# A token over two PSUM banks, six casts moved to ScalarE, three subtractions moved to GpSimd, and other banks for the row turns, in a fused attention and expert kernel

## The chip, the cores and the metric

The kernel runs on one core of one Trainium2 chip. The metric is device time in microseconds (us) of one execution. TensorE (PE) multiplies and turns tiles into PSUM, VectorE (DVE), ScalarE (ACT) and GpSimd (POOL) do the elementwise work, SyncE (SP) issues most DMAs. Each engine works through its own instructions strictly in order.

## The reference

Windowed attention over 4 batches of 576 positions and 8 heads gives 2304 rows of 512. A top-1 mixture of 8 experts works on the rows, then a dense layer.

```python
scores = scale * q @ k.T + slopes * -abs(rel)        # window of 128 back
x = softmax(scores) @ v                               # 2304 rows of 512
logits = x @ w_gate + modality_bias[modality_id]
e = argmax(logits); gate = softmax(logits)[e]
y[e == i] = gate * (maximum(x[e == i] @ w1[i], 0) @ w2[i])    # w1: 512 x 1024
r = maximum(y @ w_in, 0)                              # w_in: 512 x 2048
out = (r * r) @ w_out
```

## The kernel before

All large products run on TensorE in a split form: each fp32 operand becomes a high part (a cast to fp32r) and a low part (the operand minus the high part), and three of the four part products are added in PSUM (`passes`, L691). PSUM has 8 banks, given out by tag: two each for s, t and v, one each for x and m. Where a tag has two banks they are taken in turn, so a new tile waits until the tile before the last of that tag has been read out.

**Order.** The program is written as one stream under a manual schedule, so the order in the code is the order on each engine. Helpers written as generators are advanced one step at a time at fixed places; a `yield` in one moves what follows to a later place.

**Attention** runs in 40 units (batch, 128 queries, half of the heads). In step k, VectorE makes the scaled and biased scores of unit k (`smax`, L274 to L281), ScalarE their exponentials (L300), TensorE the scores of unit k+1 (`sc`, banks s and t, L258 or L260), the transposes of unit k-2 (`tr`, a bank of v, L322) and the products with v of unit k-3 (`pv`, bank x, L359). ScalarE reads the transposes out (`ev`, L329 to L335), and GpSimd masks them (L339, L340). After every second unit `post` copies the finished rows from bank x (ScalarE, L379), turns them back together with the gate products (TensorE, L388) and scales them (VectorE, L403).

**Routing** (`route`) handles two or three row tiles at a time in steps that are taken between `tr` and `pv`, and once more behind `pv`. Two of its steps take a v bank: the rank product (L449, L450) and the table product (L478), whose results VectorE reads at L454 and L482.

**The first slot.** After 8 of the 18 row tiles the largest expert's first 512 rows are gathered, while attention still runs (`prefetch_first`). Each of the four row tiles is turned by TensorE into a v bank (`turn`, L673); ScalarE casts it (L678), and `finish` subtracts on VectorE (L682), which frees the bank. Three of this expert's weight chunks of 128 x 1024 are split here (`wsplit`): the high part on VectorE (L617, as one cast), the low part on GpSimd (L621, as two halves). From step 40 on the expert's first products (`up_first`) are laid between the last attention units, two pieces of four matmuls in a step.

**Slots 1 to 4** follow, each with eight first products (`ffn1`), relu with split (ScalarE L715, VectorE L716), and second products (`ffn2`). During the last of them (slot 4, 384 rows) `weights(0)` prepares the dense layer's first weights by Strassen-like sums: s1, s3, s2, s4 are added on GpSimd (L820), and a11, a12, s1, a22, s3, s2, s4 are cast on ScalarE (L814) and subtracted on VectorE (L815), in that order. Then comes a loop that runs zero times here (L1122).

**The dense layer** visits three blocks of 768 rows four times (`way_up`, `way_down`). In the first two visits `turn_rows` turns the next block's six row tiles between the way up and the way down: 24 transposes of 128 x 128 (L1300), copied out by ScalarE (L1303). The way down begins with two v banks.

Of the kernel before, what the change touches and what calls it, by code (L numbers as in the profile page):

```python
# [8 lines left out]
F32 = mybir.dt.float32  # L9
# [4 lines left out]
ALU = mybir.AluOpType  # L14
# [38 lines left out]
def attention_moe_kernel(ctx, tc, qh, kh, v, mid, wg, mb, w1, w2, win, wout, out):  # L53
# [355 lines left out]
    gends = {2: 3, 5: 3, 7: 2, 10: 3, 13: 3, 16: 3, 17: 1}  # L409
    ready = []  # L410

    def route(g0, G):
        gs = slice(g0, g0 + G)
        last = g0 + G == NT
        aux = dve
        at = "m" if last else "v"
        l = l_all[:, gs, :]
        sh = [128, G, E]
        small, big = row(), row(F32R)
        used = [0, 0]  # L420

        def t(shape, which=0):
            n = 1
            for x in shape:
                n *= x
            o = used[which]
            used[which] = o + n
            v = (big if which else small)[:, o:o + n]
            return v if len(shape) == 1 else v.rearrange("p (a b) -> p a b", a=shape[0]) if len(shape) == 2 else v.rearrange("p (a b c) -> p a b c", a=shape[0], b=shape[1])

        eq, mw, oh = t([G, E]), t([G]), t([G, E], 1)
        ohf = oh.bitcast(F32)
        dve.tensor_tensor(l, l, lbias[:, gs, :], op=ALU.add)
        dve.tensor_reduce(mx_all[:, gs], l, axis=AX.X, op=ALU.max)
        yield
        dve.tensor_tensor(eq, l, mx_all[:, gs, None].to_broadcast(sh), op=ALU.is_ge)
        dve.tensor_tensor(eq, eq, rev[:, None, :].to_broadcast(sh), op=ALU.mult)
        yield
        dve.tensor_reduce(mw, eq, axis=AX.X, op=ALU.max)
        dve.tensor_tensor(oh, eq, mw[:, :, None].to_broadcast(sh), op=ALU.is_equal)  # L440
        while g0 >= CHECK and not checked:
            yield
        for i in range(G):
            aux.tensor_tensor(cum[:, g0 + i + 1, :], cum[:, g0 + i, :].bitcast(F32), ohf[:, i, :], op=ALU.add)
        yield
        if not last:
            yield
        rk_ = bank(at, (128, G, E))
        pe.matmul(rk_, upper, oh, start=True, stop=False)  # L449
        pe.matmul(rk_, ones, cum[:, gs, :], start=False, stop=True)  # L450
        yield
        rm, rank, ge, oc = t([G, E]), t([G]), t([G, NCH + 1]), t([G, NCH])
        cs, js, r, val = t([G]), t([G]), t([G]), t([G])
        dve.tensor_tensor(rm, rk_, ohf, op=ALU.mult)  # L454
        dve.tensor_reduce(rank, rm, axis=AX.X, op=ALU.add)
        yield
        dve.tensor_tensor(ge, rank[:, :, None].to_broadcast([128, G, NCH + 1]), thr[:, None, :].to_broadcast([128, G, NCH + 1]), op=ALU.is_ge)
        dve.tensor_reduce(cs, ge[:, :, 1:], axis=AX.X, op=ALU.add)
        aux.tensor_tensor(oc, ge[:, :, :NCH], ge[:, :, 1:], op=ALU.subtract)
        o2 = t([G, E, NCH], 1)  # L460
        sh = [128, G, E, NCH]
        aux.tensor_tensor(o2, ohf[:, :, :, None].to_broadcast(sh), oc[:, :, None, :].to_broadcast(sh), op=ALU.mult)
        yield
        dve.tensor_reduce(js, ge[:, :, 4:NCH:4], axis=AX.X, op=ALU.add)
        dve.scalar_tensor_tensor(r, cs, -128.0, rank, op0=ALU.mult, op1=ALU.add)
        yield
        dve.scalar_tensor_tensor(val, js, 512.0, rank, op0=ALU.mult, op1=ALU.subtract)
        dve.tensor_tensor(val, val, idc[:, gs], op=ALU.add)
        yield
        lh = row(F32R)  # L470
        for i in range(G):
            dve.tensor_scalar(lh[:, 128 * i:128 * i + 128], iota, r[:, i:i + 1], val[:, i:i + 1], op0=ALU.is_equal, op1=ALU.mult)
        yield
        if not last:
            yield
        tp = bank(at, (128, E * NCH))
        for i in range(G):
            pe.matmul(tp, lh[:, 128 * i:128 * i + 128], o2[:, i].rearrange("p e c -> p (e c)"), start=i == 0, stop=i == G - 1)  # L478
        yield
        if g0 + G == CHECK:  # L480
            dve.tensor_tensor(t_first, t_acc, tp, op=ALU.add)
        dve.tensor_tensor(t_int if last else t_acc, t_acc, tp, op=ALU.add)  # L482
        if g0 + G == CHECK:
            ready.append(first_slot())
        if last:
            ready.append(slots())
# [124 lines left out]
        rawt[key] = r = wt(side, F32)  # L611
        nc.sync.dma_start(out=r, in_=src)

    def wsplit(key, src=None, eng=None, sides=("left", "left"), quick=False):
        r = rawt.pop(key) if src is None else src
        h, l = wt(sides[0], F32R), wt(sides[1], F32R)
        (dve.tensor_copy if quick else act.copy)(h, r)  # L617
        n = 2 if eng is pool else 1
        for i in range(n):
            c = slice(1024 // n * i, 1024 // n * (i + 1))  # L620
            (eng or dve).tensor_tensor(l[:, c], r[:, c], h[:, c].bitcast(F32), op=ALU.subtract)  # L621
        W[key] = h, l
# [138 lines left out]
    def advance_split(upto):  # L761
        while pos[1] < min(upto, len(seq)):
            s, j = key = seq[pos[1]]
            wsplit(key, None, pool if s == 0 and j < 3 else None, chunk_sides(s, j), s == 0 and j < 3)
            pos[1] += 1

    convs = [(k_, i) for p in range(PASSES) for k_ in (2 * p, 2 * p + 1, 2 * p + 8, 2 * p + 9) for i in range(2)]
# [43 lines left out]
    def weights(p):  # L811
        def split(n, src):
            t = wt("left", F32R)
            act.copy(t[:, :512], src)  # L814
            dve.tensor_tensor(t[:, 512:], src, t[:, :512].bitcast(F32), op=ALU.subtract)  # L815
            dw[p][n] = [x.rearrange("p (c f) -> p c f", c=2) for x in (t[:, :512], t[:, 512:])]

        def both(a, b, op):
# [45 lines left out]
    def prefetch_first():  # L864
        index(0, column(0))
        advance_load(1)
        yield
        for i in range(0, 4):
            gather(0, i)
            yield  # L870
        advance_load(2)
        yield
        advance_load(3)
        advance_split(1)
        for i in range(4):

            yield
            while not tail[0]:
                yield
            finish = turn(0, i, xr[0][1][i], "v", later=True)  # L880
            yield
            finish()
            if i % 2:
                advance_split(2 + i // 2)
        primed.append(True)
# [407 lines left out]
    def turn_rows(j):  # L1293
        for h in range(2):
            for k in range(2):
                raw[k, h] = quarter()
        for i in range(BT):
            p = bank("xmss"[i % 4], (128, 4, 128))
            for c in range(4):
                pe.transpose(p[:, c, :], yrow(j, i)[:, 128 * c:128 * c + 128], ident)  # L1300
            t = slice(128 * (i % 3), 128 * (i % 3) + 128)
            for k in range(2):
                act.copy(raw[k, i // 3][:, :, t], p[:, 2 * k:2 * k + 2, :])  # L1303
        del yr[j]
# [163 lines left out]
```

## Time and profile before

| | |
|---|---|
| median of 3 runs | 771.26 us (767.74 to 771.78) |
| the profiled execution | 771.87 us |
| its span on the core | 770.2 us |
| TensorE busy | 739.6 us, 96% |
| VectorE, ScalarE, GpSimd busy | 504.0, 343.0, 295.8 us |

A row of the timeline gives the start in us from the span's beginning, the duration, engine, line and operation, the tile written and the tiles read, the number of merged instructions, and in brackets the engine's idle time just before, with the instruction that ended last before it resumed. Where an instruction waits for several, that name can be another than the one that mattered. The granted clock of TensorE is 1.00 at 2.4 GHz and 0.50 at 1.2 GHz.

### The profile page before, as it was taken

What the parts mean: (1) busy time and instruction counts of PE and PEld (TensorE: products, weight loads), DVE (VectorE), ACT (ScalarE), POOL (GpSimd) and SP (SyncE); (2) the same over time, 40 slices, a digit from 0 to 9 for tenths busy, and PEclk for the clock granted to TensorE, in tenths of its full rate; (3) what the DMA queues carried; (4) which work ended last, traced back from release to release, by engine and by line L of the source; (5) the groups of instructions that cost most, each with busy time, mean ns of one, the idle gap of its engine ahead of it and who ended that gap; (6) DMA issues with size and microseconds to landing.
All of it is one profiled execution on the core that took longest, in us unless ns stands there. A gap on an engine that the chain in (4) does not pass through costs nothing.

```text
span 770.2 us, 12620 instructions
## 1 busy us (share of the span) xinstructions
PE 739.6 (96%) x4183; PEld 635.4 (83%) x4183; DVE 504.0 (65%) x1274; ACT 343.0 (45%) x833; POOL 295.8 (38%) x322
## 2 busy tenths in 40 slices
PE   9999997899999999998889999999999999999997
PEld 7777765777888888897778889989989899899896
DVE  7788888788876957677374455457655677542542
ACT  6676665324434445454365564524233233231230
POOL 4322353304444543443172454136343255340431
PEclk9999999999999999999999999999999999999999
DMA  8558440238687685960486772689738797195832
GB/s 272 173 181 269 155 175 15 70 123 318 229 306 250 227 270 184 391 217 14 172 308 257 302 321 80 249 357 336 302 117 300 305 381 294 72 341 207 332 119 83
DMA packets 71156, 174.72 MB, mean 227 GB/s; under 512 B 10033, under 2 KB 18481, under 8 KB 71089
## 3 DMA queue, kind: packets, MB, share of 16 engines
q1 hardware_dynamic: 68048, 163.93, 58.8%
q0 software_dynamic: 3040, 9.96, 3.5%
q8 instruction: 34, 0.56, 0.3%
q14 instruction: 34, 0.27, 0.1%
HBM read 117.76 MB, written 56.10 MB: 226 GB/s over the span
## 4 chain that ended last, share of the span: by engine, by line
PE 48%; DVE 2%; issue 1%; ACT 1%; DVEq 0%; ACTq 0%
PE v L691 17%; PE t L691 12%; PE s L691 12%; PE x L691 3%; PE m L691 3%; DVE cr L1259 1%; DVE cr L1284 1%; DVE xq L1203 0%; PE m L1300 0%; PE x L1300 0%; ACT w L1303 0%; DVE cr L1262 0%; ACT hd L1251 0%; ACT cr L1261 0%; DVE row L1320 0%
## 5 line engine op out<-in xcount | busy, mean ns | idle before, releaser
L1252 POOL TENSOR_TENSOR hd<-cr,hd 128x384 fp32r<-128x384 f32 x96 | 112.9, 1210 | 141.0 <-ACT hd L1251 140.9
L691 PE MATMUL v<-w,hd 128*128 128x512 f32 x576 | 138.2, 392 | 0.0
L691 PEld LDWEIGHTS v<-w,hd 128*128 128x128 f32 x576 | 108.8, 189 | 22.3
L691 PE MATMUL s<-xq,w 128*128 128x384 f32 x576 | 108.1, 335 | 0.7 <-DVE cr L1284 0.7
L691 PE MATMUL t<-w,h 128*128 128x512 f32 x408 | 100.8, 400 | 3.6 <-DVE w L1158 2.1
L691 PEld LDWEIGHTS s<-xq,w 128*128 128x128 f32 x576 | 100.9, 188 | 2.1 <-issue 1.0
L643 POOL TENSOR_TENSOR row<-row 128x512 int32<-128x512 int32 x32 | 47.5, 1484 | 131.8 <-DVE row L642 75.2
L691 PEld LDWEIGHTS t<-w,h 128*128 128x128 f32 x408 | 76.3, 191 | 20.5 <-issue 2.6
L1251 ACT CAST hd<-cr 128x384 fp32r<-128x384 f32 x96 | 49.2, 513 | 66.4 <-DVE cr L1259 63.4
L691 PE MATMUL t<-w,hd 128*128 128x512 f32 x288 | 69.2, 389 | 0.0
L691 PE MATMUL s<-w 128*128 128x512 f32 (+1 forms) x292 | 67.9, 384 | 1.1 <-DVE h L716 1.1
L300 ACT ACTIVATE e<-x,m 128x128 f32<-128x128 f32 x128 | 50.3, 396 | 33.7 <-DVE m L279 33.7
L1320 DVE SCALAR_TENSOR_TENSOR row<-v,gate,row 128x512 f32<-128x512 f32 x36 | 27.0, 750 | 56.6 <-PE v L691 54.4
L691 PEld LDWEIGHTS t<-w,hd 128*128 128x128 f32 x288 | 54.1, 188 | 11.2
L691 PEld LDWEIGHTS s<-w 128*128 128x128 f32 x292 | 53.3, 188 | 11.3 <-DVE h L716 2.0
L621 DVE TENSOR_TENSOR w<-w 128x1024 fp32r<-128x1024 f32 x37 | 49.6, 1345 | 18.0 <-ACT w L617 17.9
L1281 ACT COPY cr<-s 128x384 f32<-128x384 f32 x48 | 23.0, 481 | 74.0 <-PE s L691 73.7
L1259 DVE SCALAR_TENSOR_TENSOR cr<-cr 128x384 f32<-128x384 f32 x72 | 52.5, 729 | 2.5
L339 POOL TENSOR_SCALAR_AFFINE_SELECT pt<-pt 128x512 f32<-128x512 f32 (+1 forms) x32 | 19.2, 599 | 84.8 <-ACT pt L335 65.8
L1284 DVE TENSOR_TENSOR cr<-t,cr 128x384 f32<-128x384 f32 x24 | 13.3, 554 | 44.1 <-PE t L691 44.1
L617 ACT CAST w<-w 128x1024 fp32r<-128x1024 f32 x37 | 38.7, 1049 | 2.4 <-DMA w<-w 2.3
L635 ACT ACTIVATE row<-w 128x512 f32<-128x512 f32 x32 | 21.2, 669 | 29.7 <-POOL row L643 25.7
(293 smaller groups left out, 1361.3 us busy)
## 6 DMA issues: line engine op xcount, KB each, us to landing
xq<-xs SPq DMA_DIRECT2D x42, 768.0 KB, 9.3
w<-w SPq DMA_DIRECT2D x40, 512.0 KB, 4.9
xs<-xq SPq DMA_DIRECT2D x21, 768.0 KB, 4.2
ya<-row SPq DMA_DIRECT2D x54, 256.0 KB, 3.4
row<-ya SPq DMA_DIRECT2D x54, 256.0 KB, 7.2
w<-win SPq DMA_DIRECT2D x16, 512.0 KB, 6.4
wc<-row SPq DMA_DIRECT2D x32, 256.0 KB, 2.5
w<-wout SPq DMA_DIRECT2D x16, 512.0 KB, 6.1
```

Source lines behind the costliest of these rows:

```text
L300: act.activation(e[:, i, j, :], x[:, i, j, :], AF.Exp, bias=m[:, i, j:j + 1], scale=-1.0, accum_out=rinv[b, t][:, h:h + 1])
L617: (dve.tensor_copy if quick else act.copy)(h, r)
L621: (eng or dve).tensor_tensor(l[:, c], r[:, c], h[:, c].bitcast(F32), op=ALU.subtract)
L635: act.mul(f, hi.bitcast(F32), 2.0 ** -112)
L643: pool.tensor_tensor(a, a, r, op=ALU.add)
L691: pe.matmul(ps, l, r, start=first and i == 0, stop=last and i == n - 1, **kw)
L1251: act.copy(gh, c)
L1252: pool.tensor_tensor(gl, c, gh.bitcast(F32), op=ALU.subtract)
L1259: dve.scalar_tensor_tensor(c, c, 0.0, c, op0=ALU.max, op1=ALU.mult)
L1281: act.copy(c, ps[q])
L1284: dve.tensor_tensor(c, ps[q], c, op=ALU.add)
L1320: dve.scalar_tensor_tensor(o, ps, gate, o, op0=ALU.mult, op1=ALU.add)
```

## The change

A list `vbusy` serves as a token. A routing group takes it before its rank product and before its table product and gives it back when VectorE has read the result; a first-slot turn takes it before it is written and gives it back with `finish`. Whoever finds it taken yields and tries again at the next place. Routing groups from row tile 8 on also yield once more before their table product. `turn` itself is unchanged.

The three first-slot casts go from VectorE (one of 1024 columns) to ScalarE (two of 512 columns, each ahead of the GpSimd half that reads it). The subtractions of a12, a22 and s2 of the dense layer's first weights go from VectorE to GpSimd. `turn_rows` takes the banks v, v, x, m, s, s in place of x, m, s, s, x, m.

```diff
+    vbusy = []
 def route(g0, G):
...
         if not last:
             yield
+            while vbusy:
+                yield
+            vbusy.append(g0)
         rk_ = bank(at, (128, G, E))
         pe.matmul(rk_, upper, oh, start=True, stop=False)
...
         dve.tensor_reduce(rank, rm, axis=AX.X, op=ALU.add)
         yield
+        vbusy.clear()
...
         if not last:
             yield
+            if g0 >= CHECK:
+                yield
+            while vbusy:
+                yield
+            vbusy.append(g0)
         tp = bank(at, (128, E * NCH))
...
         dve.tensor_tensor(t_int if last else t_acc, t_acc, tp, op=ALU.add)
+        vbusy.clear()
...
-    def wsplit(key, src=None, eng=None, sides=("left", "left"), quick=False):
+    def wsplit(key, src=None, eng=None, sides=("left", "left")):
         r = rawt.pop(key) if src is None else src
         h, l = wt(sides[0], F32R), wt(sides[1], F32R)
-        (dve.tensor_copy if quick else act.copy)(h, r)
         n = 2 if eng is pool else 1
+        for i in range(n):
+            c = slice(1024 // n * i, 1024 // n * (i + 1))
+            act.copy(h[:, c], r[:, c])
         for i in range(n):
             c = slice(1024 // n * i, 1024 // n * (i + 1))
             (eng or dve).tensor_tensor(l[:, c], r[:, c], h[:, c].bitcast(F32), op=ALU.subtract)
...
-            dve.tensor_tensor(t[:, 512:], src, t[:, :512].bitcast(F32), op=ALU.subtract)
+            (pool if p == 0 and len(dw[p]) % 2 else dve).tensor_tensor(t[:, 512:], src, t[:, :512].bitcast(F32), op=ALU.subtract)
...
-            while not tail[0]:
+            while not tail[0] or vbusy:
                 yield
+            vbusy.append(-1)
             finish = turn(0, i, xr[0][1][i], "v", later=True)
             yield
             finish()
+            vbusy.clear()
...
-            p = bank("xmss"[i % 4], (128, 4, 128))
+            p = bank("vvxmss"[i], (128, 4, 128))
```

**TensorE, attention step 35.** Before, the table product (v<-row) stands between the transposes and the next `post`, and the second turn (v<-ident,row) closes the step:

```order
L322 MATMUL v<-ident,e 128x128 x4
L478 MATMUL v<-row 128x160 x3
L388 MATMUL m<-turned,row 128x144 x3
L388 MATMUL x<-turned,row 128x144
L359 MATMUL x<-pt,vS 64x128 x8
L673 MATMUL v<-ident,row 128x128 x4
```

After, for the same step (L489 is the table product):

```order
L322 MATMUL v<-ident,e 128x128 x4
L388 MATMUL m<-turned,row 128x144 x3
L388 MATMUL x<-turned,row 128x144
L359 MATMUL x<-pt,vS 64x128 x8
L489 MATMUL v<-row 128x160 x3
```

The table product has moved behind `pv`; the second turn comes one step later, the third in step 37, the fourth in step 39 (before: steps 35, 36 and 37). The first pieces of `up_first` stay in step 40.

**GpSimd, slot 4, the sums and subtractions of the dense layer's first weights.** Before, the four sums s1, s3, s2, s4 and then the next scatter:

```order
L820 TENSOR_TENSOR row_4227<-w_3985 128x512
L820 TENSOR_TENSOR row_4247<-w_3983,w_3985 128x512
L820 TENSOR_TENSOR row_4278<-row_4227,w_3983 128x512
L820 TENSOR_TENSOR row_4303<-w_3983,row_4278 128x512
L726 MEMSET spacer_150 1x1
L727 DMA yd_70<-row_4425,idx_3864 2816x512
```

After (L834 the sums, L829 the subtractions of a12, a22 and s2):

```order
L834 TENSOR_TENSOR row_4230<-w_3988 128x512
L834 TENSOR_TENSOR row_4250<-w_3986,w_3988 128x512
L829 TENSOR_TENSOR w_4278<-w_3986,w_4278 128x512
L834 TENSOR_TENSOR row_4281<-row_4230,w_3986 128x512
L829 TENSOR_TENSOR w_4303<-w_3988,w_4303 128x512
L834 TENSOR_TENSOR row_4306<-w_3986,row_4281 128x512
L829 TENSOR_TENSOR w_4334<-row_4281,w_4334 128x512
L740 MEMSET spacer_150 1x1
L741 DMA yd_70<-row_4428,idx_3867 2816x512
```

One subtraction now stands ahead of the sum s2, and two ahead of the sum s4.

**TensorE, the first dense visit, end of the way up and start of the way down.** Before:

```order
L691 MATMUL s<-xq,w 128x384 x12
L1300 MATMUL x<-ident,w 128x128 x4
L1300 MATMUL m<-ident,w 128x128 x4
L1300 MATMUL s<-ident,w 128x128 x8
L1300 MATMUL x<-ident,w 128x128 x4
L1300 MATMUL m<-ident,w 128x128 x4
L691 MATMUL v<-w,hd 128x512 x12
```

After:

```order
L705 MATMUL s<-xq,w 128x384 x12
L1316 MATMUL v<-ident,w 128x128 x8
L1316 MATMUL x<-ident,w 128x128 x4
L1316 MATMUL m<-ident,w 128x128 x4
L1316 MATMUL s<-ident,w 128x128 x8
L705 MATMUL v<-w,hd 128x512 x12
```

The v banks are now written first by the turns, and the s banks last.

## Rows read from the trace of the kernel before

**Rows 1.** The page: busy time, share, instructions of each engine.

```profile
PE 739.6 (96%) x4183; PEld 635.4 (83%) x4183; DVE 504.0 (65%) x1274; ACT 343.0 (45%) x833; POOL 295.8 (38%) x322
```

**Rows 2.** Windows of 10 us: engines' busy time, PEclk, DMA share, GB/s.

```profile
110.00:120.00 10.00, 7.16 (x58) 5.17 (x57) 9.36 (x44) 7.65 (x31) 5.87 (x8) 0.98 0.41 158
120.00:130.00 10.00, 9.86 (x85) 7.97 (x86) 7.36 (x27) 3.91 (x14) 3.99 (x5) 0.85 0.08 28
130.00:140.00 10.00, 5.98 (x46) 5.09 (x43) 9.45 (x40) 5.63 (x21) 5.31 (x7) 0.84 0.07 26
...
400.00:410.00 10.00, 8.74 (x38) 6.99 (x39) 3.62 (x5) 5.77 (x17) 3.63 (x4) 0.83 0.50 207
```

**Rows 3.** Timeline of TensorE, attention steps 35 to 40, its idle times.

```profile
118.94 0.54 PE L478 MATMUL v<-row 128*128 128x160 f32 x3 [2.73 <-DVE ri L390]
...
131.47 0.66 PE L673 MATMUL v<-ident,row 128*128 128x128 f32 x4 [1.04 <-ACT pt L335]
...
136.19 0.28 PE L449 MATMUL v<-row,upper 128*128 128x24 f32 x1 [2.98 <-ACT pt L335]
...
143.29 1.09 PE L359 MATMUL x<-pt,vS 128*64 128x128 f32 x16 [1.10 <-DVE ls L403]
```

**Rows 4.** Timeline of VectorE over the same steps.

```profile
114.06 2.56 DVE L472 TENSOR_SCALAR row<-iota,row 128x128 fp32r<-128x128 f32 x3
...
118.05 0.74 DVE L682 TENSOR_TENSOR w<-v,w 128x256 fp32r<-128x256 f32 x2
...
135.21 0.75 DVE L682 TENSOR_TENSOR w<-v,w 128x256 fp32r<-128x256 f32 x2
...
144.14 0.88 DVE L472 TENSOR_SCALAR row<-iota,row 128x128 fp32r<-128x128 f32 x3
```

**Rows 5.** Groups by line: the first slot's casts (count, busy us, mean ns, idle).

```profile
L617 DVE CAST w<-w 128x1024 fp32r<-128x1024 f32 x3 | 2.1, 685 | 0.0
```

**Rows 6.** Timeline of ScalarE, attention steps 34 and 35.

```profile
113.54 0.40 ACT L300 ACTIVATE e<-x,m 128x128 f32<-128x128 f32 x1 [0.46 <-DVE m L279]
...
116.09 0.59 ACT L379 COPY row<-x 128x512 f32<-128x512 f32 x1
```

**Rows 7.** Timeline of GpSimd, the first chunk's low part.

```profile
112.73 2.52 POOL L621 TENSOR_TENSOR w<-w 128x512 fp32r<-128x512 f32 x2 [1.29 <-DVE w L617]
```

**Rows 8.** Timeline of GpSimd in slot 4: sums s1 and s3; s4.

```profile
344.17 3.97 POOL L820 TENSOR_TENSOR row<-w 128x512 f32<-128x512 f32 x2
...
349.93 1.61 POOL L820 TENSOR_TENSOR row<-w,row 128x512 f32<-128x512 f32 x1
```

**Rows 9.** Timeline of ScalarE in slot 4: cast of s4; last relu.

```profile
351.56 0.62 ACT L814 CAST w<-row 128x512 fp32r<-128x512 f32 x1 [0.93 <-POOL spacer L726]
...
355.69 0.49 ACT L715 ACTIVATE h<-m 128x384 fp32r<-128x384 f32 x1
```

**Rows 10.** Timeline of VectorE in slot 4: subtraction of s3; last three instructions.

```profile
352.00 0.68 DVE L815 TENSOR_TENSOR w<-row,w 128x512 fp32r<-128x512 f32 x1
...
358.61 1.21 DVE L850 TENSOR_TENSOR w<-w 128x1024 fp32r<-128x1024 f32 x1
359.75 0.54 DVE L716 SCALAR_TENSOR_TENSOR h<-m,h 128x384 fp32r<-128x384 f32 x1
```

**Rows 11.** Timeline of TensorE in slot 4: second products.

```profile
358.74 1.21 PE L691 MATMUL t<-w,h 128*128 128x512 f32 x4 [1.12 <-DVE w L621]
360.34 5.96 PE L691 MATMUL t<-w,h 128*128 128x512 f32 x25 [0.39 <-DVEq L1122]
```

**Rows 12.** Timeline of TensorE: first v products of dense visits 1 and 2.

```profile
403.89 4.17 PE L691 MATMUL v<-w,hd 128*128 128x512 f32 x12
...
440.15 2.09 PE L691 MATMUL v<-w,hd 128*128 128x512 f32 x8
```

**Rows 13.** Timeline of ScalarE: first copies of the turned rows, both visits.

```profile
401.88 0.64 ACT L1303 COPY w<-x 128x256 f32<-128x256 f32 x2
...
438.50 0.64 ACT L1303 COPY w<-x 128x256 f32<-128x256 f32 x2
```

More of the change, by code (lines that the diff above doesn't have):

```diff
@@ L763, in advance_split @@
             s, j = key = seq[pos[1]]
-            wsplit(key, None, pool if s == 0 and j < 3 else None, chunk_sides(s, j), s == 0 and j < 3)
+            wsplit(key, None, pool if s == 0 and j < 3 else None, chunk_sides(s, j))
             pos[1] += 1
```

## The prediction, made before the run

> **What bounds the kernel now.** Read first the share of busy time: TensorE has 96% [rows 1], so time is to be won only where TensorE waits or runs at its lower clock. The windows of 10 us show where: from 190 us on nearly all are full, and the gaps lie in attention's last part, at the end of slot 4, and around 400 us [rows 2]. In each the timelines of the engines are laid side by side: what did TensorE wait for, and which engine ended last before it?
>
> In attention's end TensorE waits 2.73, 1.04, 2.98 and 1.10 us, 7.85 in all [rows 3]. The names in the brackets mislead for the first three. The two v banks are taken in turn; the table product at 118.94 needs the bank of the first turn, and that is free when `finish` ends on VectorE at 118.05 + 0.74 = 118.79. The rank product at 136.19 needs the bank of the fourth turn, whose `finish` ends at 135.21 + 0.75 = 135.96 [rows 3, 4]. So a turn holds one of two banks for most of an attention step, because its reader stands behind a whole step's work in VectorE's order. The granted clock falls besides: over the three windows from 110 to 140 us it is 0.98, 0.85 and 0.84, a loss of 0.2 + 1.5 + 1.6 = 3.3 us against full clock [rows 2]. Before both falls TensorE had just stood still for nearly 3 us. Waits and clock together: 11.15 us is the most that this stage can give through TensorE.
>
> VectorE sets a second limit there. It is busy 9.36 + 7.36 + 9.45 = 26.17 of these 30 us [rows 2].
>
> **Part 1: token and casts.** Between the turn and the reader of its bank no other taker of v but the transposes can now come. The first wait goes, since the table product stands behind `post` and `pv`. Next in line is `post`, which waits for ScalarE's copy at 116.09. A pair of casts of 512 columns is new ahead of that copy: one takes 0.62 [rows 9], the pair about 1.13 overlapped, and ScalarE had 0.46 idle just before 113.54 [rows 6], so the copy ends about 0.7 later, near 117.4. TensorE had stopped at 118.94 - 2.73 = 116.21: a wait of 1.25 is left of 2.73. Of the waits of 1.04 and 2.98 I leave 0.75: the rank product still meets a turn's `finish`, but it comes one step behind and VectorE has less queued. Bounds are nothing and 1.04, the wait before a turn in the present trace. Of the 1.10 I leave 0.2; VectorE's scaling of `post` is no longer late. The third pair of casts stands ahead of the copy that `post` needs in step 40, which now lies on the path: a new wait of 1.05, bounds 0 and 1.13. Together 3.25 in place of 7.85, a gain of 4.6. No gap of nearly 3 us is left, so I take the 3.3 of clock as won: 7.9.
>
> VectorE must keep that pace. It loses three casts, 2.06 us [rows 5]. In 110 to 140 it can close up by 30 - (26.17 - 2.06) = 5.9 us if its other work stays as long. Some of that work shrinks, some grows: the three multiplications at 114.06 took 2.56 beside GpSimd's subtraction [rows 7], the same three at 144.14 took 0.88 [rows 4]. The GpSimd halves move, so the stretch falls on other instructions. I take 7.0, between 5.9 and 7.9. Bounds for the part: a gain of 2.1 (only the casts, if VectorE is the limit) and 11.15. The Trainium skill, "SBUF — State Buffer", section "SBUF: two separate sides", says that VectorE and GpSimd share one pair of ports as an exclusive lock, the loser waiting for the whole instruction, while ScalarE and TensorE never wait there. [...]
>
> The order of SyncE is unchanged by the change, and GpSimd issues the same gathers in the same places. From step 41 on everything is paced by TensorE, so the gain travels through the slots.
>
> **Part 2: three subtractions to GpSimd.** VectorE loses a12, a22 and s2: 0.68 each where GpSimd is idle [rows 10], about 2 us, and more where it is stretched. But GpSimd works in order. Before, the sum s4 ends at 349.93 + 1.61 = 351.54, and its cast follows on ScalarE at 351.56, with no slack [rows 8, 9]. Now two subtractions stand ahead of it, each between 1.26 (half of 2.52) and 1.98 (half of 3.97) [rows 7, 8]: the sum ends 2.5 to 4.0 later, at 354.1 to 355.5, and the cast at 354.7 to 356.1. Queued behind that cast on ScalarE are the relus of the last three first products, which TensorE's second products need. Behind s4's own subtraction on VectorE (0.68) stand two relu splits of 0.54 and three weight subtractions of 1.21, 5.4 in all, and then the last relu split [rows 10]. That one would start at 360.1 to 361.5; before it started at 359.75. TensorE waited exactly there (1.12 and 0.39), and resumed at 360.34 [rows 11]. So VectorE gets free, then stands idle for GpSimd, and the end is 0.35 to 1.75 later. I take +1.0. Bounds: -1.5, if VectorE's relief arrives first and both waits go, and +1.75 plus 1.7 for one more spell of low clock (the windows' price for one: 10 x 0.17 at 400 [rows 2]).
>
> The Trainium skill, "GPSIMD Engine Reference", section "4.1 Engine selection", advises VectorE for elementwise work and calls GpSimd about 2 times slower with two inputs. The trace shows 1.26 to 1.98 against 0.68 and agrees; by that rule alone this part is a loss, as in rival 2.
>
> **Part 3: banks of the row turns.** In the first visit the way down starts at 403.89, when the 24 transposes have ended; the last two groups had to wait until the first two were copied out of x and m. With v first, no bank is used twice. The way down then needs the first v bank, which ScalarE's first two copies free: 401.88 + 0.64 = 402.52 [rows 12, 13]. Those copies stand behind casts that do not move. The transposes into s end by about 402, since they wait for VectorE as before. Gain 403.89 - 402.52 = 1.37, less a semaphore's way: 1.3. In the second visit 440.15 - (438.50 + 0.64) = 1.0. Together -2.3. Bounds: -0.9, if the second pair of v copies is waited for too, and -4.0, if the spell of low clock in the first visit (1.7) goes as well. Its waits shrink only by some tenths, so I leave that spell in.
>
> **Sum.** -7.0 + 1.0 - 2.3 = -8.3. The profiled execution took 771.87 us, 0.6 above the median of 771.26, within the runs' 767.74 to 771.78 and a little. So 763.6 for this execution, and 763.0 for the median.
>
> **Rivals.**
> 1. *VectorE is the limit in attention's end.* It is busy 94% in two of the three windows [rows 2]. Then TensorE's bank waits turn into waits for VectorE's scores and scalings, and the first part gives little more than the casts: -2.5. -2.5 + 1.0 - 2.3 = -3.8: 767.5. Against it speaks that TensorE's waits are themselves what delays VectorE's next input.
> 2. *GpSimd's queue costs more.* Both moved subtractions at 1.98 and the gaps at the end of slot 4 close enough together for one more spell of low clock: +1.75 + 1.7, about +3.4. -7.0 + 3.4 - 2.3 = -5.9: 765.4. For it: TensorE would wait over 3 us within 5 there.
> 3. *Slower: GpSimd stretches VectorE at its new places.* One mechanism, in steps 34 to 41: each of the three GpSimd pairs (2.5 us) stretches VectorE's work by 2.56 - 0.88 = 1.7 where it falls on instructions that read and write SBUF [rows 4, 7]. If all three pairs now fall on such work that was free of it, VectorE is 5.0 longer, less 2.06 of casts: +3.0 for the stage. 771.87 + 3.0 + 1.0 - 2.3 = 773.6, or 773.0 for the median. It decides from the point at which the added stretch exceeds 2.06 and the idle time of VectorE, 30 - 26.17 = 3.8, is used up. Against it: the pairs already fall on such work before.
>
> **How the numbers follow.** A measurement of this kernel can tell about 0.5%, 3.9 us, from no change. Forecast 763.0 with 62%, rival 2 with 15%, rival 1 with 17%, rival 3 with 6%. The first two lie below 767.4 and rival 1 on that border. So faster by over 0.5%: 0.84; within it: 0.11; slower: 0.05. The forecast's own range is 759.5 to 766. The low end stays there, with both clock spells gone it would be near 759; the high end takes in rivals 2 and 1: 759.0 to 768.0.
>
> **What would show it.** Part 1 is right if the waits before the table and rank products (2.73 and 2.98) are under 1 us each, the granted clock is 1.00 through the steps 35 to 40, and the first piece of `up_first` starts 7 to 9 us earlier than before; it is wrong if VectorE is then busy without a gap and TensorE waits for scores. Two new waits of about 1 us for ScalarE's row copy should appear. Part 2 is right if ScalarE waits 2.5 to 4 us for the sum s4 and VectorE has a gap there. Part 3 is right if the way down of the first two visits starts right after ScalarE's first two copies. The forecast is wrong altogether if the gain of attention's end is given back between 150 and 190 us, at the gather for slot 1 or at the weights.

## The result and the profile after

The changed kernel took 763.79 us (median of 7 runs, 761.76 to 765.75), the kernel before 770.75 us (7 runs): ratio 0.991, interval 0.989 to 0.994. A second comparison, on the chip of the last four experiments, gave 764.71 against 768.46 us: ratio 0.995, interval 0.993 to 0.997. So the change is faster by 4 to 7 us; why the two comparisons differ by 3 us is not shown. The profiled execution took 761.76 us, span 759.8, mean granted clock 0.995.

The page's busy line of the changed kernel, to be laid beside [rows 1]:

```profile
PE 734.1 (97%) x4183; PEld 630.7 (83%) x4183; DVE 498.8 (66%) x1268; ACT 345.4 (45%) x839; POOL 299.2 (39%) x325
```

TensorE issues the same 4183 matmuls in 5.5 us less busy time: a part of the gain is a higher clock, not less work. The windows of 10 us, columns as in [rows 2]:

```profile
110.00:120.00 10.00, 9.01 (x82) 6.57 (x80) 9.76 (x45) 8.05 (x32) 5.01 (x6) 1.00 0.29 107
120.00:130.00 10.00, 9.00 (x89) 7.56 (x84) 8.72 (x49) 8.73 (x33) 6.28 (x8) 1.00 0.08 28
130.00:140.00 10.00, 8.83 (x82) 6.95 (x81) 9.49 (x33) 4.54 (x14) 5.45 (x8) 1.00 0.33 107
...
390.00:400.00 10.00, 8.61 (x39) 6.64 (x38) 4.86 (x7) 6.72 (x19) 4.98 (x5) 0.83 0.52 217
```

From 110 to 140 us the clock is 1.00 where it fell to 0.85 and 0.84, and TensorE is busy 26.8 us there in place of 23.0. VectorE is nearly full: 27.97 of 30 us. The window at 390 still has its low clock. TensorE's waits in attention's end, beside [rows 3]:

```profile
111.92 0.66 PE L687 MATMUL v<-ident,row 128*128 128x128 f32 x4
...
115.22 1.00 PE L388 MATMUL m<-turned,row 128*128 128x144 f32 x6 [0.99 <-ACT row L379]
...
127.19 0.28 PE L454 MATMUL v<-row,upper 128*128 128x24 f32 x1 [0.77 <-ACT pt L335]
132.54 1.09 PE L359 MATMUL x<-pt,vS 128*64 128x128 f32 x16 [0.17 <-DVE ls L403]
135.32 1.00 PE L388 MATMUL m<-turned,row 128*128 128x144 f32 x6 [0.57 <-ACT row L379]
138.45 1.12 PE L366 MATMUL x<-pt,vS 128*64 128x64 f32 x16 [0.43 <-DVE ls L403]
...
141.67 1.12 PE L366 MATMUL x<-pt,vS 128*64 128x64 f32 x16
```

The first and the last of these in the kernel before:

```profile
113.90 0.66 PE L673 MATMUL v<-ident,row 128*128 128x128 f32 x4
...
151.09 1.12 PE L366 MATMUL x<-pt,vS 128*64 128x64 f32 x16
```

The table product waits for nothing, the rank product 0.77 in place of 2.98, and two waits for ScalarE's row copy are new. In all 2.93 us in place of 7.85. From the start of the first turn to the start of attention's last products (L366) it takes 29.75 us in place of 37.19; below this is **the stage**. The first turn itself came at 111.92 us in place of 113.90; over all profiles, of whatever kernel, it lies between 111.9 and 113.9, so these 2 us are not the change.

At the end of slot 4, beside [rows 8 to 11]:

```profile
341.98 2.28 POOL L829 TENSOR_TENSOR w<-w 128x512 fp32r<-128x512 f32 x1
344.22 1.29 POOL L834 TENSOR_TENSOR row<-w,row 128x512 f32<-128x512 f32 x1
...
345.54 0.62 ACT L828 CAST w<-row 128x512 fp32r<-128x512 f32 x1 [2.87 <-POOL row L834]
...
346.19 1.10 DVE L829 TENSOR_TENSOR w<-row,w 128x512 fp32r<-128x512 f32 x1 [3.10 <-ACT w L828]
```

ScalarE stands 2.87 us for the sum s4, and VectorE 3.10 us behind ScalarE's cast. In the dense layer, beside [rows 12, 13]:

```profile
393.21 1.19 ACT L1319 COPY w<-v 128x256 f32<-128x256 f32 x4
393.90 1.19 PE L705 MATMUL v<-w,hd 128*128 128x512 f32 x3 [0.43 <-ACT w L1319]
...
428.97 1.19 ACT L1319 COPY w<-v 128x256 f32<-128x256 f32 x4
429.66 0.73 PE L705 MATMUL v<-w,hd 128*128 128x512 f32 x2 [0.24 <-ACT w L1319]
```

The way down starts as soon as half of the four merged copies of v (one bank's two) are done. From the first row turn to the first v product it takes 4.61 and 3.09 us in the two visits, in place of 5.92 and 4.05.

### The profile page after: what moved, and what is told of

Its sections match the earlier page's. It is cut to its first block, busy times and chain, and to the rows that moved or that the text cites. A ratio compares the mean times of both kernels' runs of the same rounds, so it can differ in the third digit from the quotient of the medians.

```text
span 759.8 us, 12624 instructions
## 1 busy us (share of the span) xinstructions
PE 734.1 (97%) x4183; PEld 630.7 (83%) x4183; DVE 498.8 (66%) x1268; ACT 345.4 (45%) x839; POOL 299.2 (39%) x325
## 4 chain that ended last, share of the span: by engine, by line
PE 48%; DVE 2%; DMA 1%; ACT 1%; issue 1%; SPq 0%; ACTq 0%; DVEq 0%
PE v L705 18%; PE s L705 12%; PE t L705 12%; PE x L705 3%; PE m L705 3%; DVE cr L1275 1%; DVE cr L1300 1%; DMA w<-yd 1%; DMA yd<-row,idx 0%; DVE xq L1219 0%; ACT w L1319 0%; DVE cr L1278 0%; ACT hd L1267 0%; ACT cr L1277 0%; SPq L1053 0%
## 5 line engine op out<-in xcount | busy, mean ns | idle before, releaser
L632 ACT CAST w<-w 128x1024 fp32r<-128x1024 f32 (+1 forms) x43 | 42.0, 989 | 1.7 <-DMA w<-w 1.7
```

The source lines that it names most:

```text
L632: act.copy(h[:, c], r[:, c])
```

## The experiments

Single executions of one kernel on one chip differ by some 2 us, as much as most parts are worth. So each run is read three ways: the median against the kernel before on the same chip; the **time at full clock**, which is span times mean granted clock, averaged over the runs; and stages from the profile. The clock is a mean over the runs. Ratios are those of the comparison, with their intervals, and can differ a little from the quotient of two medians.

Two of these readings have their limits. Span times clock counts low clock as though the whole kernel slowed down with it. Within the runs of one kernel on one chip (167 runs in all) a clock lower by 0.001 goes with a span longer by some 0.5 us, not by 0.77, and the groups scatter widely around that. So the column can take out too much. A stage is read from one execution: with attention as before (before, e3, e4) it takes 36.75 to 37.19 us, with attention as changed (the changed kernel, e5, e6, e9, e10, e12) 29.75 to 30.82.

| run | median us | ratio (95%) | clock | at full clock | stage us |
|---|---|---|---|---|---|
| *chip A:* before | 768.87 | | 0.9929 | 761.7 | 37.19 |
| e1 token alone | 767.74 | 0.9985 (0.9969 to 1.0002) | 0.9919 | 759.6 | 34.57 |
| e2 casts alone | 767.63 | 0.9979 (0.9958 to 0.9999) | 0.9944 | 761.6 | 37.19 |
| e3 subtractions alone | 772.53 | 1.0053 (1.0035 to 1.0072) | 0.9885 | 761.6 | 36.75 |
| e4 banks alone | 767.58 | 0.9982 (0.9963 to 1.0001) | 0.9918 | 759.5 | 36.90 |
| *chip B:* before | 768.24 | | 0.9945 | 762.2 | |
| e5 changed, no subtractions | 760.81 | 0.9915 (0.9897 to 0.9933) | 0.9970 | 756.9 | 30.82 |
| e6 subtractions behind s4 | 762.45 | 0.9925 (0.9909 to 0.9942) | 0.9963 | 757.3 | 30.81 |
| e7 `finish` at once | 770.68 | 1.0040 (1.0023 to 1.0058) | 0.9926 | 763.4 | 37.05 |
| e8 no low parts | 763.44 | 0.9949 (0.9932 to 0.9966) | 0.9945 | 757.6 | 29.63 |
| *chip C:* before | 768.46 | | 0.9930 | 761.5 | |
| e9 changed, again | 764.71 | 0.9951 (0.9934 to 0.9968) | 0.9940 | 758.3 | 30.39 |
| e10 token and casts | 761.86 | 0.9925 (0.9901 to 0.9948) | 0.9983 | 759.4 | 30.80 |
| e11 third casts later | 759.61 | 0.9885 (0.9866 to 0.9905) | 0.9974 | 756.3 | 28.86 |
| e12 as e5, again | 760.77 | 0.9900 (0.9881 to 0.9919) | 0.9980 | 757.6 | 30.38 |

The stage given for the kernel before is that of the first profile.

**Token alone (e1).** On the kernel before; the first yield stands ahead of the table product alone, and the token is given back as in the change:

```diff
+            if g0 >= CHECK:
+                yield
+            while vbusy:
+                yield
+            vbusy.append(g0)
...
-            while not tail[0]:
+            while not tail[0] or vbusy:
                 yield
+            vbusy.append(-1)
```

> The kernel before with the token and the extra yield of the table product alone; casts, subtractions and row-turn banks as before. Theory A (a v bank is held by the place of its reader in VectorE's order): the waits of 2.73, 1.04 and 2.98 us before the table and rank products fall below 1 us each although VectorE still has its three casts (2.06 us), the granted clock stays at 1.00 from 120 to 140 us, and from the first turn to the last product of attention the stage is 5 to 7 us shorter (with all parts it was 7.4). Whole kernel: ratio 0.991 to 0.994. Theory B (VectorE's work is the limit of this stage): the waits only change their place, the stage is 0 to 2 us shorter; ratio 0.997 to 1.000.

Neither theory's number came: the stage is 2.6 us shorter. The first table product no longer waits, but the rank product of the second group does. The window from 125 to 131 us, TensorE and VectorE:

```profile
124.77 0.69 DVE L630 CAST w<-w 128x1024 fp32r<-128x1024 f32 x1
...
129.35 0.75 DVE L694 TENSOR_TENSOR w<-v,w 128x256 fp32r<-128x256 f32 x2
...
130.33 0.28 PE L454 MATMUL v<-row,upper 128*128 128x24 f32 x1 [2.03 <-ACT pt L335]
```

Its bank is freed by `finish` (L694) at 129.35 + 0.75 = 130.10. VectorE comes to that only after a run of work without a gap, in which its own cast (L630) stands. And the clock falls right after the wait, as it did before:

```profile
130.00:140.00 10.00, 9.67 (x82) 8.34 (x83) 7.25 (x30) 5.21 (x17) 4.97 (x7) 0.83 0.22 79
140.00:150.00 10.00, 8.41 (x54) 6.22 (x53) 5.56 (x23) 0.97 (x3) 2.16 (x4) 0.83 0.08 29
```

**Casts alone (e2).** On the kernel before:

```diff
-        (dve.tensor_copy if quick else act.copy)(h, r)
         n = 2 if eng is pool else 1
+        for i in range(n):
+            c = slice(1024 // n * i, 1024 // n * (i + 1))
+            act.copy(h[:, c], r[:, c])
```

> The kernel before with the three first-slot casts on ScalarE alone (two of 512 columns each in place of one of 1024 on VectorE). Theory A (the bank's reader stands late in VectorE's order): the two waits of nearly 3 us before the table and rank products stay within 1 us of what they were, the clock still falls to 0.85 behind them, and the stage from the first turn to the last product of attention is 0 to 2.1 us shorter; ratio 0.997 to 1.000. Theory B (VectorE's work is the limit): the waits shrink to under 1.5 us each and the stage is 4 to 7 us shorter; ratio 0.991 to 0.995.

The stage takes 37.19 us, as before, and the time at full clock is that of before. (The 0.5 us that the expectation of e10 puts down to the casts was a misreading: in e2's rows the last products stood as two groups, and the second had been taken.) TensorE's waits are still 7.84 us; they have moved:

```profile
116.84 0.90 PE L480 MATMUL v<-row 128*128 128x160 f32 x3 [2.38 <-DVE ri L390]
...
134.13 0.28 PE L451 MATMUL v<-row,upper 128*128 128x24 f32 x1 [1.95 <-ACT pt L335]
...
141.52 1.09 PE L359 MATMUL x<-pt,vS 128*64 128x128 f32 x16 [2.65 <-DVE ls L403]
```

The table product still waits for a `finish`, with less ahead of it on VectorE. Theory A holds: three casts less on VectorE do not shorten the stage while the bank's order stands.

**Both (e10).** The two diffs above together, without the other parts.

> The kernel before with the first part whole: token and casts, subtractions and row-turn banks as before. Alone the token shortened the stage of attention's end by 2.6 us and the casts lengthened it by 0.5. Theory C (two limits lie over each other, the bank's order and VectorE's backlog, and each hides the other): together the stage is 6 to 7.5 us shorter, all its windows are at clock 1.00, and the whole kernel is 4.5 to 7 us faster, ratio 0.991 to 0.994. Rival (the parts simply add up, and the rest of the gain came from the other parts): 2 to 2.5 us, ratio 0.997.

Theory C's numbers came: stage 30.80 us (6.4 less), clock 1.00 from 110 to 150 us, 6.6 us less in the median. The same matmul as in e1 now waits 1.21 us:

```profile
128.87 0.28 PE L454 MATMUL v<-row,upper 128*128 128x24 f32 x1 [1.21 <-ACT pt L335]
```

The split is instructive. At full clock the token alone already gives 2.0 us and the casts none; together they give 2.1. What the pair adds is clock: 0.9983 in place of 0.9930, which over 767 us is 4.1 us less lost, 2.7 by the smaller slope of the runs. The stage says the same: e1 loses 1.7 + 1.7 us there in two windows at 0.83, e10 nothing, and without that loss e1's 34.57 would be 31.2, against 30.80. Either edit alone leaves one wait of about 2 us or more in the stage, and low clock with it.

**`finish` at once (e7).** On the kernel before:

```diff
-            finish = turn(0, i, xr[0][1][i], "v", later=True)
+            turn(0, i, xr[0][1][i], "v")
             yield
-            finish()
```

> The kernel before with one edit: VectorE's part of a first-slot turn (the subtraction that frees the bank) stands right behind the turn, and not one step later; no token, casts and banks as before. Theory A (what holds the bank is the place of that subtraction in VectorE's order): the waits of 2.73 and 2.98 us before the table and rank products fall below 1.5 us each; VectorE waits up to 1 us for ScalarE's cast at each of four turns; the stage is 1 to 4 us shorter, ratio 0.995 to 0.999. Theory B (VectorE's work is the limit): VectorE's waits for the cast add up, and the stage is 1 to 4 us longer, ratio 1.001 to 1.005.

Each theory is right in part. The bank waits shrink nearly as theory A says (1.11 and 1.53, where under 1.5 was expected, in place of 2.73 and 2.98), so it is the reader's place that holds the bank. But the kernel is 2.4 us slower, within theory B's ratio. VectorE now waits 2.02, 1.24 and 0.92 us for ScalarE's cast, and TensorE's waits are 8.34 us in all, 4.57 of them for VectorE's scores and scalings. The stage of this one profile is as long as before (37.05), neither longer nor shorter as the theories had it. It has one window at 0.83 where the kernel before lost 3.3 us of clock, so at equal clock it would be some 1.5 us longer, an estimate from these two profiles.

```profile
115.53 0.54 PE L478 MATMUL v<-row 128*128 128x160 f32 x3 [1.11 <-DVE w L682]
...
119.41 0.76 DVE L682 TENSOR_TENSOR w<-v,w 128x256 fp32r<-128x256 f32 x2 [2.02 <-ACT w L678]
...
121.17 1.09 PE L359 MATMUL x<-pt,vS 128*64 128x128 f32 x16 [0.83 <-DVE ls L403]
...
132.12 0.25 PE L449 MATMUL v<-row,upper 128*128 128x24 f32 x1 [1.53 <-DVE w L682]
...
141.35 1.09 PE L359 MATMUL x<-pt,vS 128*64 128x128 f32 x16 [2.67 <-DVE ls L403]
```

Here the bank was better left to its late reader, with the other taker sent elsewhere, than freed by a reader that stands early in a full queue.

**GpSimd beside VectorE (e8).** On the changed kernel, `wsplit` for GpSimd's chunks; this kernel leaves their low parts out:

```diff
-        for i in range(n):
+        for i in range(0 if eng is pool else n):
             c = slice(1024 // n * i, 1024 // n * (i + 1))
             (eng or dve).tensor_tensor(l[:, c], r[:, c], h[:, c].bitcast(F32), op=ALU.subtract)
-        W[key] = h, l
+        W[key] = h, (h if eng is pool else l)
```

> The changed kernel without GpSimd's subtractions for the low parts of the first slot's three weight chunks; the high part is used in the low part's place, so this part of the computation is left out. It measures what GpSimd's halves cost VectorE beside them. Theory A (TensorE paces the stage now, it was busy 9.0 us of each 10): the three multiplications of the table step fall from 2.81 us to about 0.9, VectorE is 3 to 5 us less busy from 110 to 140 us, and the stage is at most 1 us shorter. Theory B (VectorE's stretched work is the limit after the change): the stage is 3 to 5 us shorter.

The table step's multiplications, in the changed kernel and then in e8:

```profile
134.12 2.82 DVE L478 TENSOR_SCALAR row<-iota,row 128x128 fp32r<-128x128 f32 x3
...
134.35 2.51 POOL L635 TENSOR_TENSOR w<-w 128x512 fp32r<-128x512 f32 x2 [0.28 <-ACT w L632]
```

```profile
136.41 0.86 DVE L478 TENSOR_SCALAR row<-iota,row 128x128 fp32r<-128x128 f32 x3
136.90 0.60 ACT L379 COPY row<-x 128x512 f32<-128x512 f32 x1
...
137.56 1.00 PE L388 MATMUL m<-turned,row 128*128 128x144 f32 x6 [0.75 <-ACT row L379]
```

They took 2.82 us beside GpSimd; without it they take 0.86. The stage is 1.2 us shorter than e6's on the same chip and 0.1 shorter than the changed kernel's own, which is about the scatter of single profiles, and the time at full clock is no better than e5's or e6's. Theory A: GpSimd does hold VectorE up, but after the change that is mostly off the path. What is on it stands in the same rows: TensorE waits 0.75 us for the row copy, and GpSimd has no part in that.

**Third casts later (e11).** On e5, so that the third pair of casts stands behind the row copy:

```diff
         for i in range(4):
...
-            if i % 2:
-                advance_split(2 + i // 2)
+            if i == 1:
+                advance_split(2)
         primed.append(True)
+        yield
+        yield
+        advance_split(3)
```

> The changed kernel with the three subtractions back on VectorE, and besides the third pair of casts on ScalarE behind the row copy that the turned rows wait for, not ahead of it. If the wait of 0.75 us before that product in step 40 comes from the pair (1.13 us): the wait goes, GpSimd's halves of the third chunk start about 0.6 us later, which nobody waits for, and the stage is 0.5 to 0.75 us shorter than without this edit; in the whole time that is at the border of what can be told. Rival (ScalarE's backlog is not the pair alone, or VectorE's 2.8 us beside GpSimd end last there): under 0.2 us, the wait turns into one for VectorE.

The wait before the turned rows of step 40 is gone:

```profile
135.51 0.59 ACT L379 COPY row<-x 128x512 f32<-128x512 f32 x1
...
135.96 0.86 DVE L478 TENSOR_SCALAR row<-iota,row 128x128 fp32r<-128x128 f32 x3
135.99 1.14 ACT L632 CAST w<-w 128x512 fp32r<-128x512 f32 x2
136.45 0.90 PE L388 MATMUL m<-turned,row 128*128 128x144 f32 x6
136.69 2.53 POOL L635 TENSOR_TENSOR w<-w 128x512 fp32r<-128x512 f32 x2 [0.78 <-ACT w L632]
136.74 1.27 DVE L390 TENSOR_SCALAR ri<-ri 128x8 f32<-128x8 f32 x1
```

The stage is 28.86 us against 30.38 in e12 on the same chip. The 0.56 us that the pair cost is explained; the rest lies mostly in two waits behind the first turn (0.43 and 1.13 us in e12, none and 0.95 in e11), which this edit does not touch, and stays open (profiles with one and the same attention differ by up to 1.1). With 759.61 us this is the fastest kernel run: 1.2 us below e12, with overlapping intervals, but 5 us below the changed kernel, with separate ones.

**Subtractions alone (e3).** On the kernel before:

```diff
-            dve.tensor_tensor(t[:, 512:], src, t[:, :512].bitcast(F32), op=ALU.subtract)
+            (pool if p == 0 and len(dw[p]) % 2 else dve).tensor_tensor(t[:, 512:], src, t[:, :512].bitcast(F32), op=ALU.subtract)
```

> The kernel before with the three subtractions of a12, a22 and s2 on GpSimd alone. By the forecast: the sum s4 ends 2.5 to 4 us later, ScalarE waits for it, VectorE has a gap of about 3 us behind ScalarE's cast, and from the start of slot 4 to the end of the way up's first products it is 0.35 to 1.75 us longer; ratio 1.000 to 1.002. Rival (VectorE's relief arrives first): 1.5 us shorter; ratio 0.998. Rival (one more spell of low clock): 2 to 3.4 us longer; ratio 1.003 to 1.005.

Slower by 0.53%, mostly through the clock: the mean clock is 0.9885 against 0.9929, 3.4 us, and at full clock the time is that of before (-0.1 us; by the smaller slope of the runs 2.2 us of clock and +1.1). The late sum is there in e3 by itself: ScalarE waits 2.86 us for s4, VectorE's gap is 3.09. The number of the third case came, 3.7 us. Where the clock is lost is not shown: e3's one profile, at 0.991, loses as much in attention's end, behind slot 4 and at 400 us as that of the kernel before.

**Without the subtractions (e5, e12) and the changed kernel again (e9).** The edit of e5 and e12 is e3's line turned back, in the changed kernel.

> The changed kernel with the three subtractions back on VectorE; token, casts and banks as changed. Theory A (behind GpSimd's queue the sum s4 comes late, and this part costs about 0.8 us, 0.3 in slot 4 and 0.5 at the way up): ScalarE's wait of 2.87 us and VectorE's gap of 3.10 us are gone, and the time is 0.3 to 1.5 us below the changed kernel's; ratio to before 0.9895 to 0.991. Rival (this part is a gain, VectorE's relief counts): 0.5 to 2 us above the changed kernel, ratio 0.992 to 0.994.

> The changed kernel once more, on the same chip as the next three, to set the part of the three subtractions against it. Ratio 0.991 to 0.993; mean granted clock 0.993 as in its seven runs, so that the time at full clock (span times mean granted clock) is 756 to 757.5 us. If the clock of this kernel is 0.996 or more here, the cost put down to the subtractions was a difference between chips.

> The changed kernel with the three subtractions back on VectorE, once more beside the changed kernel on one chip. Theory A (the subtractions cost 0.2 us of order and about 3 us of clock, since the gaps at the end of slot 4 are followed by low clock): mean granted clock 0.996 to 0.998 against 0.993, and 2 to 3 us less than the changed kernel. Rival (they cost only the order, and the clock differed by chance): within 0.5 us of the changed kernel.

The changed kernel missed its own numbers in e9: 0.9951 for 0.991 to 0.993, and 758.3 us at full clock for 756 to 757.5. Its clock, 0.994, stays below the 0.996 that would have put the cost of the subtractions down to the chips. e5 came just short of theory A's ratio (0.9915 for 0.9895 to 0.991). On one chip, e12 is 3.9 us below the changed kernel: 0.7 at full clock, and 0.9980 against 0.9940 of clock, 3.1 us. The clock is theory A's; the time is more than its 2 to 3 us. TensorE's products at the end of slot 4, in e9 and then in e12, show the order's share:

```profile
349.25 0.73 PE L705 MATMUL t<-w,h 128*128 128x512 f32 x2 [0.33 <-ACT h L729]
350.46 0.49 PE L705 MATMUL t<-w,h 128*128 128x512 f32 x1 [0.48 <-DVE h L730]
351.52 0.49 PE L705 MATMUL t<-w,h 128*128 128x512 f32 x1 [0.56 <-ACT w L632]
353.19 1.20 PE L705 MATMUL t<-w,h 128*128 128x512 f32 x4 [1.18 <-DVE w L635]
354.80 3.58 PE L705 MATMUL t<-w,h 128*128 128x512 f32 x8 [0.40 <-DVEq L1138]
```

```profile
344.27 2.35 PE L705 MATMUL m<-w 128*128 128x384 f32 x12 [0.64 <-DVE h L730]
...
352.09 1.20 PE L705 MATMUL t<-w,h 128*128 128x512 f32 x4 [1.12 <-DVE w L635]
353.69 1.67 PE L705 MATMUL t<-w,h 128*128 128x512 f32 x6 [0.41 <-DVEq L1138]
```

Five gaps within 6 us (2.95 us) in place of three (2.17), of which one comes earlier: 0.8 us more. In e9 two spells of low clock follow in the next 20 us:

```profile
350.00:360.00 10.00, 7.39 (x22) 5.25 (x23) 4.74 (x6) 3.39 (x6) 0.99 (x1) 0.83 0.07 27
360.00:370.00 10.00, 7.86 (x28) 5.97 (x28) 1.75 (x8) 0.59 (x1) 1.15 (x3) 0.83 0.31 113
```

In e12 only the second window is at 0.83, in e5 and e10 neither; but in e11, which has no such subtractions, both. So a single profile proves nothing here. The means over the runs show that the subtractions lower the clock (e3, and e9 beside e12); that these gaps are what lowers it is argued, not shown. The window near 400 us has low clock in three of four profiles of kernels with all three parts (the changed kernel, e6, e9; not e8), and in none of those without the subtractions that have token and casts (e5, e10, e11, e12). Why the subtractions should matter for the clock at 400 stays open.

**Subtractions behind s4 (e6).** On the changed kernel:

```diff
-            (pool if p == 0 and len(dw[p]) % 2 else dve).tensor_tensor(t[:, 512:], src, t[:, :512].bitcast(F32), op=ALU.subtract)
+            if p == 0 and len(dw[p]) % 2:
+                held_back.append((t, src))
+            else:
+                dve.tensor_tensor(t[:, 512:], src, t[:, :512].bitcast(F32), op=ALU.subtract)
...
+        for t, src in held_back:
+            pool.tensor_tensor(t[:, 512:], src, t[:, :512].bitcast(F32), op=ALU.subtract)
```

> The changed kernel, but GpSimd's three subtractions stand behind its sum s4 in its order, so that the sum is as early as before and VectorE is still relieved. Theory A (the wait for s4 is what holds VectorE's last relu split, and TensorE waits for that): ScalarE's wait of 2.87 us falls below 0.5, VectorE's gap of 3.10 us below 0.5, TensorE's waits at the end of slot 4 (0.33, 0.48, 0.56 and 1.18 us) fall to 0.8 in all, and the time is 1 to 2.5 us below the changed kernel's, with the spell of low clock there gone. Rival (the rows that the way up loads are the next thing that is late: it waited 0.90 and 0.30 us for them already): slot 4 ends 1 to 2 us earlier and the way up waits as much longer; within 0.5 us of the changed kernel.

ScalarE's wait for s4 falls to 0.95 us (under 0.5 was expected) and VectorE's gap goes, as theory A says; but TensorE's last wait grows to 1.72, where 0.8 in all was expected, and the window at 350 us keeps its low clock (0.83):

```profile
343.87 0.62 ACT L830 CAST w<-row 128x512 fp32r<-128x512 f32 x1 [0.95 <-POOL row L839]
...
349.25 1.83 DVE L635 TENSOR_TENSOR w<-w 128x1024 fp32r<-128x1024 f32 x1
...
351.14 3.36 PE L705 MATMUL t<-w,h 128*128 128x512 f32 x7 [1.72 <-DVE w L635]
```

GpSimd's subtractions now lie beside VectorE's last weight splits, and one of 1.21 us takes 1.83; ScalarE besides stands 1.22 us before its next weight cast, until a GpSimd subtraction ends. With 762.45 us it lies 1.6 us above e5 on the same chip, with overlapping intervals: neither of the two places on GpSimd shows a gain over VectorE.

**Banks alone (e4).** On the kernel before:

```diff
-            p = bank("xmss"[i % 4], (128, 4, 128))
+            p = bank("vvxmss"[i], (128, 4, 128))
```

> The kernel before with the row-turn banks v, v, x, m, s, s alone. By the forecast: from the way up's last part to the first product of the way down it is 1.3 us shorter in the first visit and 1.0 us in the second, with the spell of low clock of the first visit still there: 2.3 us in all, ratio 0.997. With all parts together 0.5 of it was given back in the way up that follows; then 1.8, ratio 0.9975. Rival (the first v bank is waited for as long as the others were): under 0.5 us, ratio 1.000.

As forecast: 1.29 and 0.95 us in the two visits, 2.2 us at full clock; in the median 1.3, the rest lost to a clock of 0.9918 against 0.9929. The first product waits 0.44 us for the copy that frees its bank. The spell of low clock at 400 us, which was expected to stay, is not in e4's profile.

## Why the prediction was right, and where it was not

Forecast 763.0 us, measured 763.8 and 764.7; faster, as forecast. By its steps:

- **What holds the banks: right.** e7 shows that the reader's place holds them, e1 that the token takes the table product's wait away. The waits fall from 7.85 us to 2.93 (3.97 in e10); forecast 3.25. The two new waits for ScalarE's row copy are where they were forecast, 0.99 and 0.57 us for 1.25 and 1.05. The rank product, forecast at 0.75, waits 0.76 to 1.23: under 1 us only in part of the runs. The first piece of `up_first` is 8.8 us earlier, counted from the first turn (133.56 - 111.92 against 144.31 - 113.90), within the 7 to 9; in the profile's own time it is 10.8.
- **Part 1's size: right, -6.6 (e10) for -7.0.** By the runs' clock, 4.1 us of it are clock and 2.1 order; by the stage, 3.3 and 3.1, where the forecast took 3.3 of clock as won.
- **Rival 1 (VectorE is the limit): wrong as the whole, right as a second condition.** With the token alone VectorE's backlog is what ends last (2.03 us), and the casts alone leave the stage as long as it was. The prediction priced the casts at 2.06 us of VectorE; beside the token their worth was that the last long wait shrank, and the clock did not fall behind it. Rival 3 did not occur: where GpSimd's halves fell on VectorE's work, this cost at most 1.2 us of the stage (e8). The Trainium skill ("SBUF — State Buffer", "SBUF: two separate sides") says that VectorE, for some of its instructions, and GpSimd lock a pair of ports against each other, and that the one that starts first keeps it for its whole instruction. e11 agrees: a VectorE instruction on 8 columns, 0.16 us at 125.59, took 1.27 us beside GpSimd's pair of 2.53, about one of the two. But not every place of a pair costs VectorE something. Beside the changed kernel's second pair (125.09 us) VectorE's scores and a `finish`, which read PSUM, took their usual 0.29 and 0.75 us.
- **Part 2: the mechanism right, the size wrong.** The late sum, ScalarE's wait (2.87, forecast 2.5 to 4) and VectorE's gap came as described, and the order costs 0.8 us in TensorE's waits, 0.7 at full clock, for +1.0. The step that failed was to leave the clock out of the forecast's +1.0 and give it to rival 2 with 15%: over the runs the part costs 3.9 us (3.7 by itself, in e3), some 3 of them clock. That is rival 2's +3.4, or a little more.
- **Part 3: right.** 1.3 and 1.0 us forecast, 1.29 and 0.95 measured in e4; from e10 to e12 it is 1.8 us at full clock and 1.1 in the median, where -2.3 was forecast.
- **The sum.** On one chip -6.6 - 1.1 + 3.9 = -3.8, where -8.3 was forecast. The time still came within 2 us of 763.0, because the base lay lower: 768.2 to 768.9 us in the later comparisons, where the forecast had 771.3. So there it was met by two errors that oppose each other: the terms too favourable by 4.5 (2.9 of it part 2), the base too high by 2.8. In the first comparison both were smaller: 770.75 - 7.0, the base 0.5 too high and the terms 1.3 too favourable. That the number came so close is in part luck.

## What to carry to other kernels

When a PSUM bank is held too long, look for the place of its reader in the reader's queue, and send the other taker to a place behind it. Two limits that lie over one another (here a bank's order and a full VectorE queue) may have to be lifted together: each edit alone gave about 1 us, at the border of what can be told, both 6.6. Before work is moved to an idle engine, look at what is queued there behind it: here a sum that another engine needed at once stood behind the moved subtractions, and they cost 3.9 us.

## What the hardware showed that was not expected

The granted clock is a term of its own. The same kernel on the same chip has runs at a mean clock of 0.990 and 0.996 (e9): 766.2 us against 763.0 to 764.0. Those are 2 to 3 us, where span times clock would make 4.6. So low clock costs less than its share here, and why is not shown. Changes that differ little at full clock (e3: -0.1 us) can differ by 3 us in the median, and this shows in the mean of the runs, not in one profile.

On chip C the parts add up in every reading, because each is the difference to the next kernel there. The test is the four edits alone, on chip A. Their medians sum to nothing (-1.1, -1.2, +3.7 and -1.3), where the changed kernel gained 3.8 us in e9. At full clock they sum to -4.3 (-2.0, 0.0, -0.1 and -2.2) against -3.2, which agree within the scatter of about 1 us. That speaks for the clock as the thing through which these edits act on one another; more is not shown.
